# Three expert blocks, then three cosine blocks, with the operand differences made on GpSimd

## The chip, the cores and the metric

One core of a Trainium2 chip runs the whole program: windowed attention, a soft mixture of eight experts, and a feed-forward layer with a cosine gate. The metric is device time in microseconds (us). The engines are TensorE (PE in the rows; PEld is its weight load), VectorE (DVE), ScalarE (ACT), GpSimd (POOL) and SyncE (SP), which here issues the DMAs.

## The reference, cut to what matters

```python
# attention: B=4, H=8, S=576, D=64, causal window of 128, a slope per head
scores = np.where(mask, scale * q @ k.T + bias, -1e9)
x = softmax(scores) @ v            # reshaped to (2304, 512)
# experts: E=8, F=1024
P = np.exp(x @ w_gate - max)       # then 8 rounds: rows, columns normalised
for e in range(E):
    out += P[:, e:e+1] * (np.maximum(x @ w1[e], 0) @ w2[e])
# cosine layer: 512 -> 2048 -> 512; w_in and w_out come as float64
h = out @ w_in
return (h * np.cos(h)) @ w_out
```

## The kernel before

The 2304 tokens are three blocks (b = 0, 1, 2) of 768. A block goes through the experts in 32 units of 256 hidden columns ("moe"), and later through the cosine layer in 8 such units ("ffn"); a unit of a block is a step, and there are 120 steps. The texts call these expert blocks 0 to 2 and cosine blocks 0 to 2.

Every float32 operand is kept as a high part (a ScalarE copy rounded to the matmul's type) and a low part (what is left), and three products are summed. The front product of a unit (`g1`) is done in seven block products over halves of the operands, in the order B11, B21, T2, T1, T3, T4, B22 by the token operand that each reads (`ORDER`, `XI`). Each is six matmuls of 384 columns (`unit_mm`, L734). T1 = b12 - b11, T2 = b22 - T1, T3 = b22 - b12 and T4 = b21 - T2 are differences of quarters of the block; `combos` makes them (L264, VectorE) and splits all seven operands (L258 ScalarE, L259 VectorE) into the tiles `xt...`, of which there is one set. So the operands of the next block overwrite those of the running one, during its last step.

Within a unit the y bank accumulates four of the seven products, and is read out in between: ScalarE copies it into a snapshot (`keep`, L757) before the next product goes on accumulating; VectorE adds snapshots to the x and z banks (`add`, L760). An expert unit then applies relu and splits (L695 ScalarE, L696 VectorE); a cosine unit runs `cos_chain` over some two units' time (`tail`, one step at each `tick`), whose last operation is on GpSimd (L722). The output product (`g2`, L830 to L832) is six matmuls of 512 columns for each of six groups of 128 tokens; VectorE adds it into the block's sum (L811, L821).

The program is written out in order. The main loop goes over the steps; each step has seven positions j. At a position stand one front group, one `slot`, one output group of an earlier step with another `slot`, if one is due, and one piece of `combos` in the last step of a block. An expert step's output groups come at positions 1 to 6 of the next step; a cosine step's first comes at position 6 of the next, and its other five in the step after that. So the second unit of a cosine block holds one output group only, and the five are made up later.

Side work is fed in by slots, one piece of each list at a time: `pre` (the first block prepares the expert weights: `prep_s`, `prep_a`, `prep_b`, and stores them for the later blocks), `bg` (the normalisation of the gate; `x2_pieces`, the transposes that make a cosine block's operands from an expert block's sum; 32 times `convert_f64`, which turns a chunk of the float64 weights into float32 with seven VectorE operations, L218 to L238, and whose load buffer `u0` is single) and `bg2` (`prep_ffn`, the split of the cosine weights). Before a block's last step, `bg` and `bg2` are run to their end. In attention a list `conv` is stepped at every second group; the first block's `combos` is its last entry.

Buffers: `k0` to `k3` hold in turn a block's attention output, its expert sum, the cosine operands and the cosine sum.

## Time and profile before

| | us |
|---|---|
| median of 3 runs | 2176.64 |
| lowest and highest | 2174.65, 2178.61 |
| the profiled execution | 2179.0 |
| its span, first to last instruction | 2177.2 |

| engine | busy us | share of the span |
|---|---|---|
| TensorE | 2087.3 | 96% |
| VectorE | 1382.9 | 64% |
| ScalarE | 775.1 | 36% |
| GpSimd | 420.9 | 19% |

The share of an engine is an average over stages with different limits. The profile also gives the clock that TensorE was granted, as a share of its upper level: 1.00 is 2.4 GHz and 0.5 is 1.2 GHz; over the whole span it was 0.984. In the rows a line L734 is line 734 of the kernel above, "x6" counts instructions, and what stands in square brackets is the idle time of the engine just before the row, with who ended it.

### The profile page before, as it was taken

What the parts mean: (1) busy time and instruction counts of PE and PEld (TensorE: products, weight loads), DVE (VectorE), ACT (ScalarE), POOL (GpSimd) and SP (SyncE); (2) the same over time, 40 slices, a digit from 0 to 9 for tenths busy, and PEclk for the clock granted to TensorE, in tenths of its full rate; (3) what the DMA queues carried; (4) which work ended last, traced back from release to release, by engine and by line L of the source; (5) the groups of instructions that cost most, each with busy time, mean ns of one, the idle gap of its engine ahead of it and who ended that gap; (6) DMA issues with size and microseconds to landing.
All of it is one profiled execution on the core that took longest, in us unless ns stands there. A gap on an engine that the chain in (4) does not pass through costs nothing.

```text
span 2177.2 us, 28335 instructions
## 1 busy us (share of the span) xinstructions
PE 2087.3 (96%) x10623; PEld 1827.2 (84%) x10623; DVE 1382.9 (64%) x2497; ACT 775.1 (36%) x1544; POOL 420.9 (19%) x500
## 2 busy tenths in 40 slices
PE   8997999999999999999999499999999999899998
PEld 6665888988887888898988389888889898788897
DVE  5665866666787777777765357754545454656766
ACT  6774333333333222222223254312222222244443
POOL 4342233333332011122211212100000000022222
PEclk9998999999999999999999799999999999999999
DMA  5641567676776577878786535454444545444543
GB/s 142 156 115 66 196 247 260 240 267 240 272 271 254 200 270 289 307 280 312 290 296 232 200 153 202 169 192 177 173 199 168 205 164 209 159 169 185 189 163 117
DMA packets 162104, 456.94 MB, mean 210 GB/s; under 512 B 67504, under 2 KB 106416, under 8 KB 131248
## 3 DMA queue, kind: packets, MB, share of 16 engines
q1 hardware_dynamic: 161968, 455.15, 57.6%
q8 instruction: 83, 1.36, 0.3%
q14 instruction: 53, 0.43, 0.1%
HBM read 326.65 MB, written 128.45 MB: 209 GB/s over the span
## 4 chain that ended last, share of the span: by engine, by line
PE 79%; DVE 9%; ACT 4%; DMA 4%; POOL 3%; issue 1%; SPq 0%; POOLq 0%; ACTq 0%; DVEq 0%
PE y_moe L734 15%; PE g_moe L832 10%; PE g_moe L831 10%; PE g_moe L830 10%; PE z_moe L734 8%; PE y_ffn L734 4%; PE x_moe L734 3%; PE g_ffn L832 3%; PE g_ffn L831 3%; PE g_ffn L830 3%; PE s L427 3%; PE z_ffn L734 2%; PE x L519 2%; DMA wd<-wb 1%; ACT h_moe L695 1%
## 5 line engine op out<-in xcount | busy, mean ns | idle before, releaser
L821 DVE SCALAR_TENSOR_TENSOR acc_moe<-g_moe,prob,acc_moe 128x512 f32<-128x512 f32 x546 | 408.6, 748 | 278.4 <-PE g_moe L832 277.8
L832 PE MATMUL g_moe<-wb,h_moe 128*128 128x512 f32 x1152 | 459.7, 399 | 2.9 <-DVE h_moe L696 2.9
L830 PE MATMUL g_moe<-wb,h_moe 128*128 128x512 f32 x1152 | 451.5, 392 | 6.4 <-ACT h_moe L695 6.1
L831 PE MATMUL g_moe<-wb,h_moe 128*128 128x512 f32 x1152 | 456.4, 396 | 0.0
L757 ACT ACTIVATE s_moe<-y_moe 128x384 f32<-128x384 f32 x288 | 141.4, 491 | 687.7 <-PE y_moe L734 687.7
L734 PE MATMUL y_moe<-xtT_moe,wa 128*128 128x384 f32 x1728 | 352.7, 339 | 34.9 <-ACT s_moe L757 34.9
L734 PEld LDWEIGHTS y_moe<-xtT_moe,wa 128*128 128x128 f32 x1728 | 311.4, 190 | 62.5 <-ACT s_moe L757 38.2
L832 PEld LDWEIGHTS g_moe<-wb,h_moe 128*128 128x128 f32 x1152 | 216.8, 188 | 53.6 <-DVE h_moe L696 7.9
L722 POOL TENSOR_TENSOR h_ffn<-c_ffn,h_ffn 128x768 fp32r<-128x768 f32 x48 | 89.0, 1859 | 845.7 <-ACT h_ffn L720 813.0
L830 PEld LDWEIGHTS g_moe<-wb,h_moe 128*128 128x128 f32 x1152 | 217.6, 189 | 36.3 <-ACT h_moe L695 9.5
L695 ACT ACTIVATE h_moe<-c_moe 128x384 fp32r<-128x384 f32 x192 | 131.7, 686 | 310.3 <-DVE c_moe L760 309.4
L831 PEld LDWEIGHTS g_moe<-wb,h_moe 128*128 128x128 f32 x1152 | 216.9, 188 | 26.9
L696 DVE SCALAR_TENSOR_TENSOR h_moe<-c_moe,h_moe 128x384 fp32r<-128x384 f32 x192 | 146.8, 765 | 144.9 <-ACT h_moe L695 144.9
L120 POOL TENSOR_TENSOR s<-ra 128x256 f32<-128x256 f32 x80 | 60.5, 756 | 589.8 <-DVE wa L132 324.6
L760 DVE TENSOR_TENSOR c_moe<-z_moe,s_moe 128x384 f32<-128x384 f32 x192 | 106.9, 557 | 78.5 <-ACT s_moe L757 61.3
L734 PE MATMUL z_moe<-xtT_moe,wa 128*128 128x384 f32 x576 | 117.7, 339 | 0.0
L734 PE MATMUL y_moe<-xtB_moe,wa 128*128 128x384 f32 x576 | 116.7, 336 | 0.3
L734 PE MATMUL z_moe<-xtB_moe,wa 128*128 128x384 f32 x576 | 115.9, 336 | 0.0
L734 PE MATMUL x_moe<-xtB_moe,wa 128*128 128x384 f32 x576 | 115.8, 335 | 0.0
L830 PE MATMUL g_ffn<-wb,h_ffn 128*128 128x512 f32 x288 | 113.2, 393 | 2.3 <-DVE acc_ffn L811 2.3
L832 PE MATMUL g_ffn<-wb,h_ffn 128*128 128x512 f32 x288 | 114.5, 397 | 0.0
L811 DVE TENSOR_TENSOR acc_ffn<-g_ffn,acc_ffn 128x512 f32<-128x512 f32 x126 | 86.4, 688 | 44.2 <-PE g_ffn L832 43.4
(159 smaller groups left out, 3044.5 us busy)
## 6 DMA issues: line engine op xcount, KB each, us to landing
wa<-wd SPq DMA_DIRECT2D x88, 1792.0 KB, 8.7
wb<-wd SPq DMA_DIRECT2D x88, 1024.0 KB, 4.8
wd<-wa SPq DMA_DIRECT2D x32, 1792.0 KB, 6.8
wd<-wb SPq DMA_DIRECT2D x32, 1024.0 KB, 5.3
ra<-in_moe_w_dram SPq DMA_DIRECT2D x64, 256.0 KB, 7.4
rb<-in_moe_w_dram SPq DMA_DIRECT2D x64, 256.0 KB, 5.7
wd<-hla SPq DMA_DIRECT2D x48, 256.0 KB, 9.8
wd<-hlb SPq DMA_DIRECT2D x40, 256.0 KB, 8.4
```

What stands on the lines that cost most here:

```text
L427: nc.tensor.matmul(ps[:, x * 192 + c0:x * 192 + 192], qB[pi % 2][:, i, :], kT[pi][:, k0:k0 + w])
L695: nc.scalar.activation(out=h[:, 0, cols], in_=c, func=AF.Relu)
L696: nc.vector.scalar_tensor_tensor(out=h[:, 1, cols], in0=c, scalar=0.0, in1=h[:, 0, cols].bitcast(F32), op0=ALU.max, op1=ALU.subtract,)
L722: nc.gpsimd.tensor_tensor(out=h[:, 1], in0=c, in1=h[:, 0].bitcast(F32), op=ALU.subtract)
L734: nc.tensor.matmul(ps[:, :HB], wa[:, wl, WI[m], kc, :], x[:, xl, kc, :], start=start and kc == 0 and n_ == 0, stop=stop and kc == 1 and n_ ...
L757: nc.scalar.activation(out=snap[i], in_=y[:, :HB], func=AF.Copy)
L760: nc.vector.tensor_tensor(out=o, in0=ps[:, :HB], in1=snap[i], op=ALU.add)
L811: nc.vector.tensor_tensor(out=a, in0=ps, in1=a, op=ALU.add)
L821: nc.vector.scalar_tensor_tensor(out=a, in0=ps, scalar=pe, in1=a, op0=ALU.mult, op1=ALU.add)
L830: nc.tensor.matmul(ps, hf[f][:, 0, ts], wb[:, 0, f, :], start=f == 0, stop=False)
L831: nc.tensor.matmul(ps, hf[f][:, 0, ts], wb[:, 1, f, :], start=False, stop=False)
L832: nc.tensor.matmul(ps, hf[f][:, 1, ts], wb[:, 0, f, :], start=False, stop=f == 1)
```

## The change

The phases run in the order expert 0, 1, 2, cosine 0, 1, 2; before it was expert 0, 1, cosine 0, expert 2, cosine 1, 2. The buffers of sums and cosine operands follow. The differences move from VectorE to GpSimd, into a generator `stages` of their own: T1 and T2 are made four steps ahead of a block's end (a list `feed`), T3 and T4 together, right behind the split of T1, in place of T1 and T2. In attention, `stages` starts at group 46 and the splits at group 54, one piece at every group. The lists `bg` and `bg2` are not run to their end any more; only `feed` is. All 32 conversions are queued after the first step of expert block 1, where they follow each other without a break; before, one was queued at every step of that block, and six in the last twelve steps of block 0. The eight `prep_ffn` start every five steps, at steps 37 to 72.

```diff
+        def stages(b, src):
...
+            def stage(nm, i, x, y, over=None):
+                if over:
+                    t = st[over]
+                elif b in (("ffn", 1), ("ffn", 2)):
+                    t = rawp.tile([P, 4, P, 2], F32, tag=("ra", "rb")[i], name=f"st{nm}_{b[0]}{b[1]}")
+                    t = t.rearrange("p a f c -> p (a f c)")[:, :TB].rearrange("p (k f) -> p k f", k=2)
+                else:
+                    t = u_pool.tile([P, 2, HB], F32, tag=("u1", "u2")[i], name=f"st{nm}_{b[0]}{b[1]}")
+                nc.gpsimd.tensor_tensor(out=t, in0=x, in1=y, op=ALU.subtract)
+                st[nm] = t
+
+            stage("T1", 0, b12, b11)
+            yield
+            yield
+            stage("T2", 1, b22, st["T1"])
+            st["rest"] = lambda: (stage("T3", 0, b22, b12, "T1"), stage("T4", 1, b21, st["T2"], "T2"))
+            yield
+
+        def combos(b, src):
...
+            for nm in ("B11", "B21", "T2", "T1", "T3", "T4", "B22"):
...
                 nc.scalar.activation(out=t[:, 0], in_=s, func=AF.Copy)
                 nc.vector.tensor_tensor(out=t[:, 1], in0=s, in1=t[:, 0].bitcast(F32), op=ALU.subtract)
                 xt[b, nm] = t
-            def stage(i, x, y):
...
-                nc.vector.tensor_tensor(out=t, in0=x, in1=y, op=ALU.subtract)
...
+                if nm == "T1":
+                    st["rest"]()
+                yield
...
-            if n == 50:
-                conv.append(combos(("moe", 0), xr[0], u_pool, ("u0", "u1")))
+            if n == 46:
+                early.append(stages(("moe", 0), xr[0]))
+            if n == 54:
+                early.append(combos(("moe", 0), xr[0]))
+            if early and next(early[0], StopIteration) is StopIteration:
+                early.pop(0)
...
-        phases = [("moe", 0), ("moe", 1), ("ffn", 0), ("moe", 2), ("ffn", 1), ("ffn", 2)]
+        phases = [("moe", 0), ("moe", 1), ("moe", 2), ("ffn", 0), ("ffn", 1), ("ffn", 2)]
...
         def slot():
             step_all(pre)
+            step_all(feed)
             step_all(bg)
             step_all(bg2)
...
-            if nxt and nxt[0] == "ffn" and to_end == 3:
-                bg.append(x2_pieces(nxt[1]))
+            if nxt and to_end == 4:
+                if nxt[0] == "ffn":
+                    feed.append(x2_pieces(nxt[1]))
+                    feed.append(lazy(lambda nxt=nxt: stages(nxt, x2r[nxt[1]])))
+                else:
+                    feed.append(stages(nxt, xr[nxt[1]]))
             nx = None
             if last and nxt:
-                while bg or bg2:
-                    step_all(bg)
-                    step_all(bg2)
-                nx = combos(nxt, xr[nxt[1]] if nxt[0] == "moe" else x2r[nxt[1]], tp2, ("c1", "c2"))
+                while feed:
+                    step_all(feed)
+                nx = combos(nxt, xr[nxt[1]] if nxt[0] == "moe" else x2r[nxt[1]])
...
-            if kind == "moe" and (b == 1 or b == 0 and u >= 20 and u % 2) and chunk < 4 * NU2:
-                bg.append(convert_f64(chunk))
-                chunk += 1
-            if (kind, b) == ("moe", 1) and u >= 4 and (u % 4 == 0 or u == NU1 - 2):
-                bg2.append(prep_ffn(NU1 + (u - 4) // 4 + (u == NU1 - 2)))
+            if (kind, b) == ("moe", 1) and u == 0:
+                bg += [convert_f64(c) for c in range(4 * NU2)]
+            at = n - NU1
+            if 0 < at <= 5 * NU2 and at % 5 == 0:
+                bg2.append(prep_ffn(NU1 + at // 5 - 1))
```

The first place is ScalarE between the end of attention and the first unit of expert block 0. `lT` belongs to the gate, `xt...` are the split operands, `s1` is the unit's first snapshot. Before:

```order
L292 ACTIVATE lT4_2859<-gate4_2854 128x384
L292 ACTIVATE lT5_2866<-gate5_2861 128x384
L258 ACTIVATE xtB21_moe0_2878<-xr0_84 128x768
L258 ACTIVATE xtT2_moe0_2885<-st1_moe0_2883 128x768
L258 ACTIVATE xtT1_moe0_2888<-st0_moe0_2881 128x768
L258 ACTIVATE xtT3_moe0_2893<-st0_moe0_2891 128x768
L258 ACTIVATE xtT4_moe0_2898<-st0_moe0_2896 128x768
L258 ACTIVATE xtB22_moe0_2901<-xr0_84 128x768
L757 ACTIVATE s1_moe0_0_2952<-y_moe0_0_2941 128x384
```

And in the changed kernel:

```order
L299 ACTIVATE lT4_2883<-gate4_2878 128x384
L299 ACTIVATE lT5_2890<-gate5_2885 128x384
L773 ACTIVATE s1_moe0_0_2950<-y_moe0_0_2939 128x384
L773 ACTIVATE s2_moe0_0_2971<-y_moe0_0_2939 128x384
L325 ACTIVATE prob_80<-logits_81,nm_2975 128x144
```

The six splits that stood between the gate and the first snapshot are gone from there; they now stand among attention's groups.

The second place is VectorE in the last unit of expert block 2, before which the operands of a cosine block are made (before: cosine 1, now: cosine 0). `st` and `stT` are the differences, `c` the sums of snapshot and bank, `h` the relu's low half, `acc` the evacuated output. Before:

```order
L259 TENSOR_TENSOR xtB_ffn_16648<-x2r_16341,xtB_ffn_16648 128x768
L821 SCALAR_TENSOR_TENSOR acc_moe_13141<-g_moe_30_2_16657,prob,acc_moe_13141 128x512
L264 TENSOR_TENSOR st_ffn_16665<-x2r_16341 128x768
L264 TENSOR_TENSOR st_ffn_16667<-x2r_16341,st_ffn_16665 128x768
L259 TENSOR_TENSOR xtT_ffn_16669<-st_ffn_16667,xtT_ffn_16669 128x768
L760 TENSOR_TENSOR c_moe_31_16605<-z_moe_31_16603,s_moe_31_16680 128x384
L696 SCALAR_TENSOR_TENSOR h_moe_31_16679<-c_moe_31_16605,h_moe_31_16679 128x384
L821 SCALAR_TENSOR_TENSOR acc_moe_13141<-g_moe_30_3_16685,prob,acc_moe_13141 128x512
L259 TENSOR_TENSOR xtT_ffn_16693<-st_ffn_16665,xtT_ffn_16693 128x768
L696 SCALAR_TENSOR_TENSOR h_moe_31_16679<-y_moe_31_16601,h_moe_31_16679 128x384
L821 SCALAR_TENSOR_TENSOR acc_moe_13141<-g_moe_30_4_16704,prob,acc_moe_13141 128x512
L264 TENSOR_TENSOR st_ffn_16712<-x2r_16341 128x768
```

And in the changed kernel:

```order
L285 TENSOR_TENSOR xtB_ffn_15537<-x2r_15110,xtB_ffn_15537 128x768
L837 SCALAR_TENSOR_TENSOR acc_moe_11883<-g_moe_30_2_15546,prob,acc_moe_11883 128x512
L285 TENSOR_TENSOR xtT_ffn_15554<-stT_ffn_15244,xtT_ffn_15554 128x768
L776 TENSOR_TENSOR c_moe_31_15494<-z_moe_31_15492,s_moe_31_15565 128x384
L712 SCALAR_TENSOR_TENSOR h_moe_31_15564<-c_moe_31_15494,h_moe_31_15564 128x384
L837 SCALAR_TENSOR_TENSOR acc_moe_11883<-g_moe_30_3_15570,prob,acc_moe_11883 128x512
L285 TENSOR_TENSOR xtT_ffn_15578<-stT_ffn_15225,xtT_ffn_15578 128x768
L712 SCALAR_TENSOR_TENSOR h_moe_31_15564<-y_moe_31_15490,h_moe_31_15564 128x384
L837 SCALAR_TENSOR_TENSOR acc_moe_11883<-g_moe_30_4_15591,prob,acc_moe_11883 128x512
L285 TENSOR_TENSOR xtT_ffn_15599<-stT_ffn_15225,xtT_ffn_15599 128x768
L776 TENSOR_TENSOR c_moe_31_15493<-z_moe_31_15492,s_moe_31_15527 128x384
```

The three difference rows are off VectorE; the splits stand at the same places as before, between the same evacuations, and the split of T3 still stands ahead of the second add.

## Rows read from the trace of the kernel before

**Rows 1.** The page's first part: busy time, share of the span, instructions of TensorE.
```profile
PE 2087.3 (96%) x10623; PEld 1827.2 (84%) x10623; DVE 1382.9 (64%) x2497; ACT 775.1 (36%) x1544; POOL 420.9 (19%) x500
```

**Rows 2.** Who waited for whom, TensorE: total us, times, longest.
```profile
PE y_moe L734 <- ACT s_moe L757: 34.9, 7, 27.2
```

**Rows 3.** Stretches: length, each engine's busy us (instructions), clock, DMA share, GB/s.
```profile
1481.14:1840.86 359.72, 359.72 (x1796) 323.46 (x1795) 185.81 (x276) 76.81 (x139) 0.00 (x0) 1.00 0.47 185
182.50:205.06 22.56, 11.64 (x49) 10.46 (x49) 13.25 (x23) 6.78 (x11) 0.00 (x0) 0.70 0.07 24
553.63:667.86 114.23, 112.34 (x548) 98.00 (x546) 87.03 (x130) 41.20 (x71) 39.11 (x35) 1.00 0.74 266
683.50:726.04 42.54, 36.05 (x157) 30.27 (x156) 32.14 (x47) 13.22 (x21) 2.98 (x1) 0.92 0.54 198
1198.80:1278.60 79.80, 44.53 (x206) 38.55 (x204) 32.10 (x45) 26.11 (x47) 18.94 (x23) 0.81 0.51 183
1356.80:1395.97 39.17, 34.73 (x157) 30.44 (x156) 32.33 (x42) 18.35 (x27) 7.64 (x4) 0.91 0.41 150
1874.85:1926.21 51.36, 43.72 (x205) 37.83 (x204) 32.09 (x45) 18.38 (x29) 3.61 (x2) 0.93 0.44 172
2007.35:2045.74 38.39, 33.55 (x157) 29.46 (x156) 30.97 (x41) 18.77 (x27) 7.64 (x4) 0.96 0.41 153
```

**Rows 4.** Timeline, expert block 2 to cosine 1: start, length, engine, operation, idle before.
```profile
1885.04 0.96 DVE L264 TENSOR_TENSOR st_ffn<-x2r,st_ffn 128x768 f32<-128x768 f32 x1
...
1886.04 0.84 ACT L258 ACTIVATE xtT_ffn<-st_ffn 128x768 fp32r<-128x768 f32 x1 [5.18 <-DVE st_ffn L264]
...
1887.31 1.31 PE L734 MATMUL y_moe<-xtT_moe,wa 128*128 128x384 f32 x6 [1.52 <-ACT s_moe L757]
1887.78 0.55 DVE L760 TENSOR_TENSOR c_moe<-z_moe,s_moe 128x384 f32<-128x384 f32 x1
...
1890.07 0.95 DVE L259 TENSOR_TENSOR xtT_ffn<-st_ffn,xtT_ffn 128x768 fp32r<-128x768 f32 x1
...
1896.28 0.50 PE L830 MATMUL g_moe<-wb,h_moe 128*128 128x512 f32 x1 [1.74 <-ACT h_moe L695]
...
1900.78 0.69 PE L734 MATMUL y_ffn<-xtT_ffn,wa 128*128 128x384 f32 x1 [2.12 <-ACT s_ffn L757]
```

**Rows 5.** Timeline, last unit of cosine block 1: a VectorE product beside GpSimd.
```profile
2013.12 0.95 DVE L717 TENSOR_TENSOR c_ffn<-c_ffn,ta 128x768 f32<-128x768 f32 x1
...
2015.08 1.85 POOL L722 TENSOR_TENSOR h_ffn<-c_ffn,h_ffn 128x768 fp32r<-128x768 f32 x1 [10.11 <-ACT h_ffn L720]
2015.46 2.29 DVE L717 TENSOR_TENSOR c_ffn<-c_ffn,ta 128x768 f32<-128x768 f32 x1
```

**Rows 6.** Timeline, a float64 conversion's third-last operation, and the next load.
```profile
1000.20 0.69 DVE L234 SCALAR_TENSOR_TENSOR fb<-f,fb 128x512 f32<-128x512 uint32 x1
...
1000.92 0.88 SPq L203 DMA_DIRECT2D f<-in_moe_w_in_dram  x2
```

**Rows 7.** One line's instructions: issue to landing of L209's loads.
```profile
DMA to landing us min/median/max: 3.5/5.6/6.9
```

**Rows 8.** The same for L203's loads.
```profile
DMA to landing us min/median/max: 2.8/4.5/8.0
```

**Rows 9.** Timeline, attention: GpSimd and the matmul behind it.
```profile
88.30 2.36 POOL L145 TENSOR_TENSOR wb<-rb,wb 128x1024 fp32r<-128x1024 f32 x1
...
91.11 0.33 PE L482 MATMUL pt<-ident,pe 128*128 128x128 f32 x1 [0.54 <-POOL pe L469]
```

**Rows 10.** Timeline, front groups, relu's low half and its first reader.
```profile
977.16 1.21 PE L734 MATMUL y_moe<-xtB_moe,wa 128*128 128x384 f32 x6
...
977.44 0.96 DVE L696 SCALAR_TENSOR_TENSOR h_moe<-c_moe,h_moe 128x768 fp32r<-128x768 f32 x1 [0.91 <-ACT h_moe L695]
...
978.20 1.20 PE L734 MATMUL x_moe<-xtB_moe,wa 128*128 128x384 f32 x6
...
979.70 0.40 PE L832 MATMUL g_moe<-wb,h_moe 128*128 128x512 f32 x1
```

More of the change, by code (lines that the diff above doesn't have):

```diff
@@ L250, in tile_attention_moe_cos_ffn @@
         xt = {}
-        def combos(b, src, pool, tags):
+        stg = {}
+        def stages(b, src):
             b11, b12 = src[:, 0:2, :HB], src[:, 0:2, HB:]
             b21, b22 = src[:, 2:4, :HB], src[:, 2:4, HB:]
-            def split(nm, s):
+            st = {}
+            stg[b] = st
+            def stage(nm, i, x, y, over=None):
[15 more added lines that the diff above has]
+        def combos(b, src):
+            st = stg[b]
+            b11, b21, b22 = src[:, 0:2, :HB], src[:, 2:4, :HB], src[:, 2:4, HB:]
+            for nm in ("B11", "B21", "T2", "T1", "T3", "T4", "B22"):
+                s = {"B11": b11, "B21": b21, "B22": b22}.get(nm)
+                s = st[nm] if s is None else s
                 t = xtp.tile([P, 2, 2, HB], F32R, tag=f"xt{nm}", name=f"xt{nm}_{b[0]}{b[1]}")
@@ L260, in split @@
                 xt[b, nm] = t
-            def stage(i, x, y):
-                t = pool.tile([P, 2, HB], F32, tag=tags[i], name=f"st{i}_{b[0]}{b[1]}")
-                nc.vector.tensor_tensor(out=t, in0=x, in1=y, op=ALU.subtract)
-                return t
-            split("B11", b11)
-            yield
-            split("B21", b21)
-            yield
-            t1 = stage(0, b12, b11)
-            t2 = stage(1, b22, t1)
-            split("T2", t2)
-            yield
-            split("T1", t1)
-            yield
-            split("T3", stage(0, b22, b12))
-            yield
-            split("T4", stage(0, b21, t2))
-            yield
-            split("B22", b22)
-            yield
+                if nm == "T1":
+                    st["rest"]()
+                yield
         def gate_block(j, pool, sb):
@@ L592, in tile_attention_moe_cos_ffn @@
         conv = []
+        early = []
         NGR = len(groups)
@@ L642, in tile_attention_moe_cos_ffn @@
                 next_half += 1
-        for c in conv:
+        for c in conv + early:
             for _ in c:
@@ L662, in blk_tile @@
             return (blk2 if tag == "k3" else blk).tile(shape, F32, tag=tag, name=name)
-        phases = [("moe", 0), ("moe", 1), ("ffn", 0), ("moe", 2), ("ffn", 1), ("ffn", 2)]
-        acc_tag = {("moe", 0): "k3", ("moe", 1): "k0", ("ffn", 0): "k3", ("moe", 2): "k1",
-                   ("ffn", 1): "k0", ("ffn", 2): "k2"}
-        x2_tag = {0: "k1", 1: "k2", 2: "k3"}
+        phases = [("moe", 0), ("moe", 1), ("moe", 2), ("ffn", 0), ("ffn", 1), ("ffn", 2)]
+        acc_tag = {("moe", 0): "k3", ("moe", 1): "k0", ("moe", 2): "k1",
+                   ("ffn", 0): "k3", ("ffn", 1): "k0", ("ffn", 2): "k1"}
+        x2_tag = {0: "k2", 1: "k2", 2: "k2"}
         accs, x2r = {}, {}
-        bg, bg2, pre = [], [], []
+        bg, bg2, pre, feed = [], [], [], []
         def step_all(lst):
@@ L673, in step_all, with lazy @@
                 lst.pop(0)
+        def lazy(f):
+            yield from f()
         def slot():
             step_all(pre)
+            step_all(feed)
             step_all(bg)
@@ L866, in tile_attention_moe_cos_ffn @@
         bg.append(sinkhorn((p_m, "m"), skp))
-        chunk = 0
         load_f64(0)
```

## The prediction

> **What bounds the kernel now.** I read the page's first part, then who TensorE waits for, then a table of stretches cut at the starts of units, and then single boundaries on the timeline. TensorE is busy for 96% of the span [rows 1], so what can be won is the rest and whatever runs at the lower clock. A unit is 7 front groups and 6 output groups of six matmuls each. In the undisturbed part of the third expert block, 23 units take 359.72 us and TensorE is never idle [rows 3]: 15.64 us each. This is the floor, and nothing in the change touches it. The largest wait [rows 2] says what it waits for: 34.9 us on a snapshot that ScalarE copies out of the y bank, 27.2 of it at one place.
>
> The stretches [rows 3] price each place as its length less 15.64 per unit. Where a stretch holds the second unit of a cosine block, that unit has 1 output group and not 6; the five are done later, at 1.39 us each (15.64 less 7 front groups of 1.04 [rows 10], over 6), so 6.95 is added to the excess. Block 0 to 1: 42.54 - 31.28 = 11.3. Block 1 to cosine 0: 79.80 - 46.92 + 6.95 = 39.8. Cosine 0 to block 2: 39.17 - 31.28 = 7.9. Block 2 to cosine 1: 51.36 - 46.92 + 6.95 = 11.4. Cosine 1 to 2: 38.39 - 31.28 = 7.1. Together 77.5 us. Two more: the first unit takes 22.56 us, with TensorE busy for 11.64 at a mean clock of 0.70; and seven late units of expert block 0, where the float64 conversions start, take 114.23 - 109.48 = 4.8 too much.
>
> **The change, part by part.** All sums are against the profiled execution: span 2177.2, 2179.0 with what lies around it, which is 2.4 above the median of the runs, 2176.64.
>
> *Start of expert block 0.* Before, six of the seven operand splits and all four differences stand between attention's last ScalarE copy and the first snapshot; after, none does, as the first fence of the section on the change shows. The first unit then has 7 x 1.04 = 7.3 us of matmuls, the small ones of the normalisation, and one wait for a snapshot: I take 9.0, which needs the clock to stay at its upper level. Gain 13.6 (11 if the clock falls, 14.5 at best).
>
> The same work now runs inside attention: 7 copies of 0.84 on ScalarE, 7 differences of 0.95 on VectorE, and 4 GpSimd operations as long as the 1.85 us one of the same shape [rows 5]. Attention's normalisation is on GpSimd, and its matmuls wait for it: behind a 2.36 us GpSimd operation TensorE waited 0.54 us [rows 9]. T1 and T2 come alone, so 0.3 each. T3 and T4 come back to back, 3.7 us, of which 1.8 is hidden as there: 2. The splits I put at 0.2 each. Cost 4 (0 to 8).
>
> *Conversions out of expert block 0.* The 4.8 us go. Two GpSimd differences come into its 29th unit, behind the weight preparation: cost 1 (0 to 2).
>
> *Boundaries.* The flush is gone: the second preparation list starts at every fifth step, the last at step 72, and the cosine blocks begin at step 96, so nothing is left to flush. For the rest I replay block 2 to cosine 1 [rows 4]. Before, ScalarE stood 5.18 us at the T2 split, waiting for two VectorE differences; the snapshot behind it came late and TensorE idled 1.52. With T1 and T2 ready the two differences (0.95 each) and the copy of T2 (0.84) are no longer ahead of that snapshot, the add behind it (1887.78) comes 2.8 us earlier, and T1's split ends at 1891.02 - 2.8 = 1888.2. From there T3 is not faster: GpSimd takes 1.85, to 1890.2; ScalarE's copy 0.84, to 1891.1; but T4 holds GpSimd from 1890.2 to 1892.0. VectorE operations with both inputs in SBUF wait for a running GpSimd one: 0.95 us became 2.29 beside it [rows 5]. So T3's split runs 1892.0 to 1893.0, the add behind it to 1893.6, and ScalarE's relu to 1894.4. TensorE wants that at about 1892.9 (1896.28 less both gaps, and 0.1 for the ends that overlap): 1.5 idle, 0.5 more for the low half, and 0.5 for the next snapshot behind the splits of T4 and B22. That is 2.5 where there were 5.4.
>
> The Trainium skill, "SBUF — State Buffer", section "Who interferes with whom", states that a VectorE instruction with two SBUF inputs and a GpSimd instruction that reads SBUF exclude each other for the whole instruction. The trace agrees where it shows such a pair (0.95 against 2.29). Without this rule T3's split would start 0.9 earlier, and the five boundaries would cost 4.5 us less than I sum.
>
> The clock is the other part. Of the excess of 11.4 there, 51.36 - 43.72 = 7.6 is idle and the rest is the stretch at half clock (0.93 on average) [rows 3]. With gaps of 1.5 and 0.5 I expect half of that, 1.8. So 4.5 for block 0 to 1; 5 for block 1 to 2, where four GpSimd operations of a weight preparation stand ahead of T3; 6.5 for block 2 to cosine 0, which keeps the 2 us (7.6 - 5.4, rounded down) that a cosine block's thin second unit idles. Before, there were two such entries.
>
> Cosine to cosine, T2's split waits only for ScalarE's copy behind it, so the long snapshot wait nearly goes; VectorE's split still waits for the GpSimd half of the cosine, which holds the second half of the z bank for about 1 us. I take 2 each. Sum after: 20 (8 to 34). Gain 57.5.
>
> *Conversions in expert block 1.* 32 of them run end to end, one in 10 slots of the 13 in a unit, where there was one per unit. VectorE has room, but a conversion's first operation waits for its load, and the buffer is single. The load goes out when the third-last operation ends (1000.20 + 0.69, issued 1000.92) [rows 6]; the next first operation is due five slots on, 5 x 15.64 / 13 = 6.0 us from that operation's start, so 5.3 after the issue. Half of the chunks' loads land after 5.6 us in the middle and 6.9 at most, the others, in two pieces, after 4.5 and 8.0 [rows 7, 8]. VectorE will stand 0.3 us typically, 2.7 at worst, and behind it stand the evacuation and the adds. In the tightest place the low half is ready at 978.40 and wanted at 979.70: 1.3 us of slack [rows 10]. Most waits fit: cost 2 (0 to 6). The GpSimd differences in the middle of the cosine blocks delay VectorE once or twice: 1 (0 to 3). SyncE issues the same loads and stores as before, spread over expert blocks 1 and 2.
>
> **Sum.** -13.6 + 4 - 4.8 + 1 - 57.5 + 2 + 1 = -67.9; 2179.0 - 67.9 = 2111.1 profiled, 2.4 less as a median: **2109 us**. With all lower ends -88.8 (2088), with all upper ends -40.3 (2136).
>
> **Rivals.** *Clean boundaries* (20%): TensorE never waits for T3, the clock stays up, and attention hides the splits. Boundaries at 8 and attention at 2: 14 less, 2095. For it: both waits of ScalarE on T1 and T2 are gone, and only T3's chain is left. Against: the replay's 1.5 us behind T3.
>
> *Port-bound boundaries* (19%): every expert boundary keeps a clock drop and costs 8.5, a cosine one 5, so 37.5 with the thin unit instead of 20, and attention costs 8: 21.5 more, 2130. For it: T3 and T4 back to back block VectorE for 3.7 us where four differences took 3.8.
>
> *The work is not really ahead* (3%): prepared cosine weights are late and TensorE stops once for as long as the old flush, 27.2 us: 2136. Against: 20 units lie between.
>
> *Slower* (4%): VectorE waits for the float64 loads in expert block 1 at every conversion. Of each wait 1.3 us is slack; 31 waits eat the 68 us gained when each is 3.5 us, so from a landing of 8.8 us on. At 9.5 the wait is 4.2, and 31 x 2.9 = 90: 2109 - 2 + 90 = 2197. Against: 8.0 is the longest landing of all, with the 16 DMA engines three quarters busy late in block 0 (0.74, third of [rows 3]).
>
> **How the numbers follow.** 54% for the forecast, with its own range 2101 to 2120. The range for 8 in 10 takes in the clean case and most of the port-bound one: 2092 to 2130. Differences under 0.2% (4 us) cannot be told from none here. All cases but one end far below 2172, so faster 0.95, same 0.01, slower 0.04.
>
> **What would show it.** Right: no wait of TensorE above 5 us but the start; first unit near 9 us; no clock drop at the start of block 0; seven late units of block 0 at 15.64; at the expert boundaries no ScalarE wait on T2, and a TensorE gap of 1 to 2 us at the first output group behind the boundary, with VectorE's T3 split starting as GpSimd's T4 ends. Wrong: units of block 1 above 16 us with VectorE idle ahead of the conversion's first operation; attention longer by over 8 us; a boundary that idles as long as before.

## The result, and the profile after

The changed kernel takes 2155.15 us (median of 4 runs, 2153.53 to 2160.14) beside 2176.09 for the kernel before: a ratio of 0.9906, 95% interval 0.9887 to 0.9925. It is 21 us shorter (under 1%) where 68 were forecast, and lies outside the range of 2092 to 2130. The profiled execution has a span of 2154.0, so 23.2 of the span are gone and not 67.9.

The first part of the page after, for [rows 1]: TensorE is idle for less, 69 us in place of 90.

```profile
PE 2084.9 (97%) x10623; PEld 1816.9 (84%) x10623; DVE 1351.5 (63%) x2473; ACT 771.0 (36%) x1544; POOL 470.1 (22%) x524
```

Who TensorE waits for, for [rows 2] (total us, times, longest). The wait of 27.2 on the snapshot is gone. In its place stand many short waits, most of them for the relu and for the add that empties the z bank.

```profile
PE g_moe L846 <- ACT h_moe L711: 18.1, 14, 2.8
PE z_moe L750 <- DVE c_moe L776: 11.5, 10, 4.2
```

The stretches after, for [rows 3], in this order: the last seven units of expert block 0; its first unit; block 0 to 1; units 5 to 26 of block 1; block 1 to 2; block 2 to cosine 0; cosine 0 to 1; cosine 1 to 2. Columns as there: length, each engine's busy time, granted clock, DMA share, GB/s.

```profile
579.65:689.13 109.48, 109.48 (x547) 98.40 (x546) 71.33 (x106) 43.11 (x72) 39.61 (x35) 1.00 0.67 245
190.65:199.76 9.11, 8.53 (x50) 7.84 (x49) 4.12 (x13) 2.90 (x6) 0.00 (x0) 1.00 0.01 2
673.49:708.60 35.11, 33.38 (x157) 29.40 (x156) 24.00 (x32) 13.31 (x21) 6.07 (x3) 0.95 0.59 217
755.78:1143.19 387.41, 359.42 (x1717) 310.17 (x1716) 270.16 (x466) 83.93 (x177) 52.94 (x60) 0.99 0.72 263
1221.39:1257.82 36.43, 33.40 (x157) 29.40 (x156) 23.96 (x31) 13.34 (x25) 11.84 (x11) 0.95 0.57 217
1729.71:1774.79 45.08, 41.06 (x206) 36.34 (x205) 29.28 (x41) 19.59 (x30) 7.28 (x4) 1.00 0.50 197
1855.91:1891.09 35.18, 32.48 (x157) 27.84 (x156) 28.90 (x37) 18.78 (x27) 11.28 (x6) 1.00 0.48 174
1987.84:2023.01 35.17, 32.49 (x157) 27.83 (x156) 28.90 (x37) 18.77 (x27) 11.28 (x6) 1.00 0.47 173
```

Read as before, each length less 15.64 per unit. The seven late units have no excess, and nor have units 23 to 29, the stretch that [rows 3] has. The first unit takes 9.11. The boundaries cost 3.8, 5.2, 5.1 (45.08 - 46.92 + 6.95), 3.9 and 3.9, together 21.9. The fourth row is the surprise: 22 units take 387.41 where 22 x 15.64 = 344.08 would do, and TensorE is idle for 28.0 of it. Six units behind it, once the conversions are done, are at 15.64 again.

The sum over the places: attention 8.15 longer (it ends at 190.65 and not at 182.50), the first unit 13.45 shorter, the late units 4.8, the boundaries 55.6, block 1 42.7 longer (43.6 of excess, 0.9 before). That is -23.0, beside -23.2 measured.

VectorE's own waits from 690 to 1240 point to the cause. The first two are a conversion's first operation waiting for its float64 load, the third its fifth operation, which waits until the store before has left its buffer. Before, no conversion waited for either.

```profile
DVE fa L218 <- DMA f<-in_moe_w_in_dram: 31.8, 9, 6.7
DVE fa L218 <- DMA f<-in_moe_w_out_dram: 21.1, 7, 8.8
DVE fb L230 <- DMA w<-fb: 18.9, 6, 4.3
```

One such place on the timeline (start, length, engine, operation, idle before). SyncE issues 2.8 MB of weights (wb and wa), the raw weights of a cosine unit (ra and rb, four loads of 256 KB), and only then the float64 load. The load landed at 806.39, 11.8 us after its issue, and VectorE stood 8.79 us for it. The next add of the output and the one that empties the z bank stood behind.

```profile
791.03 0.32 SPq L109 DMA_DIRECT2D wb<-wd  x1
791.40 0.43 SPq L109 DMA_DIRECT2D wa<-wd  x1
791.88 1.22 SPq L88 DMA_DIRECT2D ra<-w  x2
793.15 0.96 SPq L88 DMA_DIRECT2D rb<-w  x2
794.55 0.33 SPq L209 DMA_DIRECT2D f<-in_moe_w_out_dram  x1
...
806.49 0.43 DVE L218 TENSOR_SCALAR fa<-f 128x512 int32<-128x512 int32 x1 [8.79 <-DMA f<-in_moe_w_out_dram]
```

Two more places that the prediction spoke of. At block 0 to 1, ScalarE no longer waits for T2, and T3's chain is what ends last: GpSimd makes T3 and T4 one after the other, VectorE's split of T3 takes 1.71 beside T4, and the gap at the first output group is 1.46.

```profile
686.97 1.85 POOL L267 TENSOR_TENSOR stT_moe<-xr 128x768 f32<-128x768 f32 x1 [8.25 <-DVE xtT_moe L285]
688.78 1.86 POOL L267 TENSOR_TENSOR stT_moe<-xr,stT_moe 128x768 f32<-128x768 f32 x1
689.74 1.71 DVE L285 TENSOR_TENSOR xtT_moe<-stT_moe,xtT_moe 128x768 fp32r<-128x768 f32 x1 [1.72 <-ACT xtT_moe L284]
...
692.85 0.50 PE L846 MATMUL g_moe<-wb,h_moe 128*128 128x512 f32 x1 [1.46 <-ACT h_moe L711]
```

In attention the same two operations stand ahead of the softmax's normalisation (L476), and TensorE waits 4.21 for it. The granted clock fell to its lower level during that wait (0.51 on average from 138 to 145).

```profile
134.02 1.80 POOL L267 TENSOR_TENSOR stT_moe<-xr 128x768 f32<-128x768 f32 x1 [1.81 <-DVE ars L470]
135.78 1.80 POOL L267 TENSOR_TENSOR stT_moe<-xr,stT_moe 128x768 f32<-128x768 f32 x1
...
137.57 1.64 POOL L476 TENSOR_SCALAR pe<-pe,arr 128x192 f32<-128x192 f32 x1
...
139.26 0.48 PE L489 MATMUL pt<-ident,pe 128*128 128x128 f32 x1 [4.21 <-POOL pe L476]
```

### The profile page after: what moved, and what is told of

Same layout as the page of the kernel before. It is cut to its first block, busy times and chain, and to the rows that moved or that the text cites. A ratio compares the mean times of both kernels' runs of the same rounds, so it can differ in the third digit from the quotient of the medians.

```text
span 2154.0 us, 28332 instructions
## 1 busy us (share of the span) xinstructions
PE 2084.9 (97%) x10623; PEld 1816.9 (84%) x10623; DVE 1351.5 (63%) x2473; ACT 771.0 (36%) x1544; POOL 470.1 (22%) x524
## 5 line engine op out<-in xcount | busy, mean ns | idle before, releaser
L120 POOL TENSOR_TENSOR s<-ra 128x256 f32<-128x256 f32 x80 | 59.5, 743 | 717.0 <-DMA ra<-w 401.8
L750 PEld LDWEIGHTS z_moe<-xtB_moe,wa 128*128 128x128 f32 x576 | 103.5, 191 | 23.9 <-DVE c_moe L776 16.5
L846 PE MATMUL g_ffn<-wb,h_ffn 128*128 128x512 f32 x288 | 113.0, 392 | 2.3 <-DVE acc_ffn L827 2.3
```

The lines of the kernel that those rows point to most:

```text
L120: nc.gpsimd.tensor_tensor(out=s4[:, o], in0=x, in1=y, op=op)
L750: nc.tensor.matmul(ps[:, :HB], wa[:, wl, WI[m], kc, :], x[:, xl, kc, :], start=start and kc == 0 and n_ == 0, stop=stop and kc == 1 and n_ ...
L846: nc.tensor.matmul(ps, hf[f][:, 0, ts], wb[:, 0, f, :], start=f == 0, stop=False)
```

## The experiments

### What makes expert block 1 longer

**One conversion per unit.** Theory A: the loads come too late for end-to-end conversions. B: the new order of the phases. C: the density of VectorE's work. In the new order a conversion's two work tiles become the staging tiles of expert block 2 from unit 29 on, so 27 conversions fit in block 1 and five follow in block 2.

```diff
-            if (kind, b) == ("moe", 1) and u == 0:
-                bg += [convert_f64(c) for c in range(4 * NU2)]
+            if kind == "moe" and (b == 1 and u < 27 or b == 2 and 1 <= u < 6):
+                bg.append(convert_f64(u if b == 1 else 26 + u))
```

> The changed kernel with the conversions one per unit again (27 in the units 1 to 27 of expert block 1, the last 5 in units 2 to 6 of expert block 2); everything else as changed. In the changed kernel block 1 took 547.9 us, 43.6 of it above 15.64 per unit in its units 3 to 25, and VectorE stood 53 us at the first operation of conversions, waiting for float64 loads, and 19 us at the fifth, waiting for the store before. Theory A (end-to-end conversions come back to the single float64 buffer before the load has landed, and VectorE stands there with adds and evacuations queued behind it): with 13 slots per conversion VectorE gets there 9.5 us after the load's issue, loads land after 3.5 to 8.4, so no wait is left; block 1 takes 505 (boundary 3.8 and at most 1), total 2113 (2108 to 2118). Rival B (phase order: block 1 loses its time to weight preparation or loads that now stand in it, not to conversions): block 1 stays above 535, total 2145 to 2155. Rival C (density of VectorE work itself) also gives 2113 here; the other runs tell it from A.

2114.48 (2112.2 to 2116.73), ratio 0.9713 (0.9692 to 0.9734). Block 1 takes 502.7. Its 22 units at the place of the row above, one row of the same view:

```profile
755.74:1099.82 344.08, 344.08 (x1718) 309.27 (x1717) 251.98 (x419) 87.09 (x176) 48.51 (x60) 1.00 0.77 281
```

Not one idle moment in 344.08 us, with DMA engines that are busier than in the changed kernel (0.77, 0.72). B falls. A and C both forecast this; the next runs tell them apart.

**The end-to-end conversions alone, in the kernel before.**

```diff
-            if kind == "moe" and (b == 1 or b == 0 and u >= 20 and u % 2) and chunk < 4 * NU2:
-                bg.append(convert_f64(chunk))
-                chunk += 1
+            if (kind, b) == ("moe", 1) and u == 0:
+                bg += [convert_f64(c) for c in range(4 * NU2)]
```

> The kernel before with one part of the change alone: all 32 float64 conversions end to end from the first unit of expert block 1, none in block 0; phase order, flush and operand differences as before. Theory A and rival C: the late units of block 0 lose their 4.8 us of excess, block 1 grows by about 40 us in its first 25 units, VectorE waits for float64 loads by about 50 us in total: 2212 (2200 to 2222). Rival B (the loss needs the new phase order): block 1 stays as before, 2170 to 2175.

2209.63 (one run), slower than before by 34, as A and C have it. VectorE's waits appear with it, in a kernel where all else is as before:

```profile
DVE fa L218 <- DMA f<-in_moe_w_in_dram: 25.7, 7, 5.9
DVE fa L218 <- DMA f<-in_moe_w_out_dram: 19.8, 9, 5.0
DVE fb L230 <- DMA w<-fb: 18.1, 6, 5.5
```

**No float64 loads but the first.** The other 31 loads are left out, and all conversions work on the first chunk.

```diff
+            if c:
+                f64_t[c] = f64_t[c - 1]
+                return
             raw = u_pool.tile([P, 512, 2], I32, tag="u0", name=f"f64_{c}")
 ...
-            raw = f64_t.pop(c)
+            raw = f64_t[c]
```

> The changed kernel with only the first float64 chunk loaded: the other 31 loads are left out, and every conversion works on the first chunk's data (so the weights of the cosine blocks are not the reference's). All operations on VectorE and all stores stay, end to end in 10 slots. Theory A: no wait at the first operation, at most a few for the stores; units of block 1 at 15.64 to 16, its excess falls from 43.6 to 5 (0 to 10), total 2116 (2110 to 2121). Rival C (density itself, VectorE busy for 75 per cent of block 1): excess stays above 30, total 2141 to 2153.

2121.45 (one run). TensorE is idle for 4.0 us from 709 to 1127, and block 1 takes 512.2, 9.4 more than with one conversion per unit. So of the 43 us the density costs at most 9, and in those there is still the wait for the store:

```profile
709.00:1127.00 418.00, 414.02 (x2049) 367.79 (x2048) 318.85 (x540) 100.14 (x203) 57.76 (x66) 1.00 0.66 243
```

```profile
DVE fb L233 <- DMA w<-fb: 13.0, 6, 3.8
```

C falls as the main cause. VectorE is busy for 318.85 of 418 us there, and that alone does not stop TensorE. In units 1 to 30 of block 1 the excess is 7.9 us beside 13.0 of waits for the store; in the changed kernel it is 43.6 beside 71.8 of waits (31.8 + 21.1 + 18.9). Both are about 0.6 us of time for each us that VectorE waited, so hardly anything is left for density to explain.

**Eleven slots in place of ten.**

```diff
             load_f64(c + 1)
             yield
             yield
+            yield
```

> The changed kernel with one empty slot more per conversion between the load's issue and the next conversion's first operation: 11 slots in place of 10, still end to end. Theory A: VectorE comes to the first operation about 1.2 us later after the load's issue (median 4.6 to about 5.8; loads land after 3.5 to 11.8, median 5.4), and has 1.2 us more per conversion to recover; the waits fall to less than half of 72 us, and the excess of block 1 from 43.6 to 15 (8 to 25): total 2126 (2118 to 2138). Rival C (density of VectorE work): the work per unit falls by one eleventh, excess 39, total 2150 (2145 to 2155).

2146.65 (2145.13 to 2148.37), where A had 2126 (up to 2138) and C 2150 (2145 to 2155): the time is in C's range and misses A's. The waits fell from 71.8 to 48.3 us, not to less than half:

```profile
DVE fb L230 <- DMA w<-fb: 18.3, 6, 7.0
DVE fa L218 <- DMA f<-in_moe_w_out_dram: 16.7, 6, 6.7
DVE fa L218 <- DMA f<-in_moe_w_in_dram: 13.3, 5, 4.6
```

The run without the loads leaves C no such cost, so A lacked something: why some loads land so late. I set each load's landing beside the time since the last 1.8 MB weight load was issued. In the changed kernel 16 loads went out less than 6.5 us behind one, and landed after 7.2 us on average and 11.8 at most; 30 went out later and landed after 4.3 on average. With one conversion per unit all 46 went out 7.4 to 8.0 behind one. The weight load itself took 8.7 to 12.1 us to land there. Conversions of 10 or 11 slots drift against units of 13, and meet the weight load again and again, at places where more of it is still to come.

**The loads on another queue.** Is it SyncE's queue, where the load stands behind the weights, or the DMA engines that both share?

```diff
-                    nc.sync.dma_start(
+                    nc.gpsimd.dma_start(
 ...
-                nc.sync.dma_start(out=raw.rearrange("p n t -> p (n t)"), in_=w_out[r0:r0 + P, :])
+                nc.gpsimd.dma_start(out=raw.rearrange("p n t -> p (n t)"), in_=w_out[r0:r0 + P, :])
```

> The changed kernel (conversions end to end, 10 slots) with one thing moved: the float64 loads are issued from GpSimd's queue in place of SyncE's. Theory A2, formed on the runs so far: end-to-end conversions drift against the units, and a load that SyncE issues less than 6.5 us after a unit's 1.8 MB weight load lands behind that, after 7.2 us on average and up to 11.8, where one issued later lands after 4.3 (16 and 30 loads of the changed kernel); at one per unit every load went out 7.4 to 8.0 us after the weight load. On a queue of its own it need not stand behind: landing at most 7, VectorE's waits for loads fall from 53 to 20 or less, total 2127 (2115 to 2140). Rival F (not the queue but the 16 DMA engines, busy with the weights, make the load late): landings and waits as in the changed kernel, total 2148 to 2160.

2170.57 (one run), worse than the changed kernel and above both forecasts. The loads that start less than 6.5 us behind a weight load (23 now) land after 7.7 on average and 11.4 at most, from a queue of their own; the others after 4.9. That is 2.9 later for the near ones, as on SyncE's queue. VectorE waits longer:

```profile
DVE fa L218 <- DMA f<-in_moe_w_in_dram: 56.1, 12, 7.7
...
DVE fa L218 <- DMA f<-in_moe_w_out_dram: 30.6, 10, 6.4
```

VectorE waits for no store in this run: 86.7 us of waits, all for loads, go with an excess of 59.1 in units 1 to 30. So late loads alone are enough. The queue falls as the main cause. What is left is the time of the start. The Trainium skill, "DMA: Bandwidth & Descriptors", section "Issuing engines are not separate DMA queues", says that transfers run on the same 16 engines and interleave, whichever engine starts them; this run agrees (7.2 and 7.7).

**The same rate at another phase.** One conversion per unit, each begun 9 slots later in its unit.

```diff
             if (kind, b) == ("moe", 1) and u == 0:
-                bg += [convert_f64(c) for c in range(4 * NU2)]
+                bg.append(pause(9))
+            if kind == "moe" and (b == 1 and u < 26 or b == 2 and 1 <= u < 7):
+                bg.append(convert_f64(u if b == 1 else 25 + u))
```

(pause yields 9 times; each conversion has three empty slots at its end, so that it fills a unit.)

> The kernel with one conversion per unit (2114.5), with every conversion begun 9 slots later in its unit, at the same rate (13 slots each). There the float64 loads went out 7.4 to 8.0 us behind a weight load's issue and landed after 4.9 on average, 7.9 at most. Theory F2 (formed on the queue's run: a float64 load that starts while a 1.8 MB weight load is under way shares the 16 DMA engines with it and lands late, from whatever queue): now most go out 2 to 6 us behind it, and land after 6.5 to 7.5 on average, 10 to 12 at most; VectorE gets there after 9.5, so waits of VectorE stay under 10 us in total and the time under 2120. Rival C2 (loads are late because VectorE's work is dense, not for where they start): landings as in the one-per-unit kernel, 4.5 to 5.5 on average.

2114.76 (one run). Of 46 loads 37 now go out 4.8 to 5.8 us behind the weight load. These land after 6.9 on average, the other nine after 5.0, all together after 6.5; with the first phase it was 4.9. Issue to landing of L203's and L209's loads in this kernel (the longest with the first phase were 7.5 and 7.9):

```profile
DMA to landing us min/median/max: 3.3/5.9/10.1
DMA to landing us min/median/max: 5.3/6.2/10.1
```

VectorE gets there 8.7 us after the issue in the middle, so it waits 3.4 us in all and the time stays. C2 falls: phase makes the landing late, and the short way from load to use makes that cost.

The weight load is not the whole of it. Where the four raw loads of a cosine unit stand between it and the float64 load, that one lands later still: after 8.9 on average here (8 of the 37 loads; 6.4 for the other 29), and after 10.1 in the changed kernel (3 of 16; 6.5 for the other 13). On GpSimd's queue they made no difference (7.7 for the 3 loads behind them, 7.7 for the other 20), so for this part the common queue may count. No run moved the raw loads alone.

### What the boundaries and attention wait for

All six start from the kernel with one conversion per unit (2114.48; profiled span 2110.6, attention until 190.5, boundaries 22.0).

**T4 one step later.**

```diff
-                if nm == "T1":
-                    st["rest"]()
+                if nm in ("T1", "T3"):
+                    st[nm + "rest"]()
```

(T1rest makes T3, T3rest makes T4.)

> The kernel with one conversion per unit (2114.5), with T4's difference issued one step later than T3's, so that in attention the normalisation of another group stands between the two on GpSimd. Theory D (attention loses its time because two differences back to back, 3.6 us, hold GpSimd while TensorE waits for the normalisation behind them, and the clock falls): the 4.2 us wait of TensorE there becomes 2.4 or less, no fall of the clock, attention 4.5 shorter (2 to 6). At the block boundaries GpSimd has nothing between the two, so T4 still follows T3 at once and VectorE's split of T3 still takes 1.7: boundaries unchanged. Total 2110 (2108 to 2113). Rival G (the two also come apart at the boundaries, since the later place in the program holds T4 back): the split takes 0.95, five boundaries give 1.5 each as well, 2103.

2112.25 (2111.81 to 2112.62). Attention ends at 190.3: D falls in this form. TensorE's first wait became shorter (1.23), but at the next group it waited 2.84 for a softmax operation that stood behind VectorE's split of T3, which took 2.48 beside T4. At the boundaries T4 still follows T3 at once and the split takes 1.70, as expected: GpSimd has nothing else there, and a later place in the program holds nothing back.

**T3 and T4 on VectorE.**

```diff
-                nc.gpsimd.tensor_tensor(out=t, in0=x, in1=y, op=ALU.subtract)
+                (nc.vector if over else nc.gpsimd).tensor_tensor(out=t, in0=x, in1=y, op=ALU.subtract)
 ...
+                if nm == "T4":
+                    st["T4go"]()
 ...
                 if nm == "T1":
-                    st["rest"]()
+                    st["T1go"]()
```

(T1go makes T3, T4go makes T4.)

> The kernel with one conversion per unit (2114.5), with T3 and T4 made by VectorE (T3 right behind T1's split, T4 at its own split), T1 and T2 ahead on GpSimd as changed. Theory P (at a boundary the end is set by T3: GpSimd's 1.85, ScalarE's copy, then a VectorE split that stands while GpSimd makes T4): T3 takes 0.95, its split 0.95 in place of 1.7, so it ends 1.6 earlier (3.5 at block 1 to 2, where four weight preparations stand ahead on GpSimd); TensorE's gap of 1.5 to 3.3 at the first output group goes or stays under 0.5, each expert boundary costs 0.5 to 2 and each cosine one 2 to 3, together 12 in place of 22; attention is 6.5 shorter, with no GpSimd operation of 1.8 behind which the normalisation stands. Total 2098 (2093 to 2104). Rival V (VectorE is short at the boundary: the differences that it makes push the relu's low half and the adds back by as much): boundaries 20 to 24, total 2106 to 2110.

2118.38 (2118.01 to 2122.6): slower, where 2098 was expected, and above V's 2106 to 2110 too. Block 1 to 2 shows why:

```profile
1200.65 0.50 PE L849 MATMUL g_moe<-wb,h_moe 128*128 128x512 f32 x1 [1.10 <-ACT h_moe L714]
...
1203.15 0.84 ACT L287 ACTIVATE xtT_moe<-stT_moe 128x768 fp32r<-128x768 f32 x1 [2.55 <-DVE stT_moe L267]
...
1205.16 1.33 PE L753 MATMUL y_moe<-xtT_moe,wa 128*128 128x384 f32 x3 [2.31 <-ACT s_moe L776]
```

The wait behind T3 fell from 3.3 to 1.1, but ScalarE now stood 2.55 for T4, and the snapshot behind it came late: 2.31. A wait was exchanged for another. Attention ended at 194.8, with 3 us of it lost before the first edited operation, part of that at another fall of the clock (0.79 from 110 to 115, where the kernel that it starts from has 1.00); those 3 us are not the edit's.

**T3 on VectorE, T4 on GpSimd already behind T2's split.**

```diff
-                nc.gpsimd.tensor_tensor(out=t, in0=x, in1=y, op=ALU.subtract)
+                (nc.vector if nm == "T3" else nc.gpsimd).tensor_tensor(out=t, in0=x, in1=y, op=ALU.subtract)
 ...
-                if nm == "T1":
-                    st["rest"]()
+                if nm in ("T1", "T2"):
+                    st[nm + "go"]()
```

(T1go makes T3, T2go makes T4.)

> The kernel with one conversion per unit (2114.5), with T3 made by VectorE right behind T1's split, and T4 by GpSimd already behind T2's split (issued ahead of T1's step). With both on VectorE the first wait behind a boundary was gone (1.45 to 0, 3.32 to 1.10), but T4 stood 2.5 us ahead of ScalarE's copy and the next snapshot came 2.3 late. Theory P2: with T4 ready early neither wait is left; the boundaries cost 14 in place of 22 and the total is 2106 (2102 to 2110). Rival V2 (T4 on GpSimd now holds VectorE's split of T1, as it held T3's before): the wait only moves, boundaries 20 to 22, 2111 to 2115.

2108.27 (2107.72 to 2110.16), ratio 0.9695 (0.9673 to 0.9718): the fastest kernel here, 47 us under the changed one. The boundaries cost 1.3, 4.9, 4.1, 3.5 and 4.5, together 18.3, where 14 was expected. At block 0 to 1 the gap is down from 1.45 to 0.52. At block 1 to 2 two weight preparations (L120) stand ahead of T4, so that T4 starts just ahead of VectorE's split of T1, which takes 2.65 in place of 0.95 and ends 0.83 behind T4. V2 holds there. Attention ends at 188.4, 2.1 earlier, and the first unit takes 10.7, 1.6 more.

```profile
1187.50 1.85 POOL L267 TENSOR_TENSOR stT_moe<-xr,stT_moe 128x768 f32<-128x768 f32 x1
1187.53 2.65 DVE L286 TENSOR_TENSOR xtT_moe<-stT_moe,xtT_moe 128x768 fp32r<-128x768 f32 x1
...
1195.09 0.50 PE L847 MATMUL g_moe<-wb,h_moe 128*128 128x512 f32 x1 [2.60 <-ACT h_moe L712]
```

**One step in every second group of attention**, and this together with the last:

```diff
-            if early and next(early[0], StopIteration) is StopIteration:
+            if early and n % 2 == 0 and next(early[0], StopIteration) is StopIteration:
```

> The kernel with one conversion per unit (2114.5), with one step of the differences and splits of expert block 0 in every second group of attention in place of every group. Attention ends at 190.5 there and at 182.5 before. Theory S (seven splits and four differences in neighbouring groups take VectorE, ScalarE and GpSimd more than the slack of the softmax chain, TensorE idles and the clock falls behind it): spread over twice the groups most of it fits, attention ends at 185 (183 to 187), total 2109 (2106 to 2112). Rival H (each step costs what it costs, wherever it stands, since the chain has no slack): attention 189 to 192, total 2112 to 2116.

> Both edits: T3 on VectorE with T4 early on GpSimd, and the spread in attention. They act in different places, so by P2 and S the gains add: 2101 (2097 to 2106). By V2 and H none is left: 2112 to 2116.

2112.93 (2111.71 to 2115.98) and 2110.04 (2108.22 to 2110.88): attention ends at 192.0 and 190.5. H holds, spreading gains nothing, and both edits together miss the 2101 that P2 and S had. TensorE's waits in the first of the two stand at the splits, for a softmax operation of VectorE (L446) that stands behind one, and once, in the last row, behind T3 and T4 on GpSimd:

```profile
127.80 0.92 PE L434 MATMUL s<-kT,qB 128*128 128x192 f32 x4 [1.29 <-DVE anb L446]
133.10 0.92 PE L434 MATMUL s<-kT,qB 128*128 128x192 f32 x4 [0.93 <-DVE anb L446]
137.92 0.44 PE L398 MATMUL T<-ident,qr 128*128 128x128 f32 x2 [0.96 <-DVE anb L446]
142.72 0.92 PE L434 MATMUL s<-kT,qB 128*128 128x192 f32 x4 [0.62 <-DVE anb L446]
145.55 0.33 PE L489 MATMUL pt<-ident,pe 128*128 128x128 f32 x1 [1.70 <-POOL pe L476]
```

**The splits behind attention again**, with T1 and T2 alone inside it.

```diff
-            if n == 54:
-                early.append(combos(("moe", 0), xr[0]))
 ...
-        for c in conv + early:
+        for c in conv + early + [combos(("moe", 0), xr[0])]:
```

> The kernel with one conversion per unit (2114.5), with the seven splits of expert block 0 and its T3 and T4 put back behind attention; only T1 and T2 stay ahead, inside it. Spread or not, on GpSimd or VectorE, attention has ended at 188 to 192 with all of them inside it, and TensorE waits 0.6 to 1.3 us at several of the splits for a softmax operation that stands behind one on VectorE. Theory S2 (each split costs attention about 0.9, T3 with T4 the rest): attention ends at 184 (183 to 185.5), 6 earlier; the first unit, with T1 and T2 ready, takes 18 (16 to 21) in place of 9.1; total 2117 (2114 to 2121). Rival H2 (it is T1 and T2, or weight preparation met at another time, that make attention longer): attention still ends at 188 or later, total 2120 to 2126.

2115.37 (2111.58 to 2116.91). Attention, and then the first unit, in the view of stretches:

```profile
0.00:182.98 182.98, 171.44 (x1172) 119.02 (x1172) 109.12 (x555) 128.81 (x430) 82.65 (x188) 0.99 0.53 136
182.98:202.79 19.81, 12.26 (x49) 10.74 (x50) 11.00 (x20) 7.36 (x12) 3.57 (x2) 0.66 0.00 1
```

S2 holds: T1 and T2 cost attention 0.5, the splits with T3 and T4 the other 7.5. Moving them ahead saves 10.7 in the first unit and costs 7.5 in attention, 3 net in these profiles; the medians of the two kernels (2115.37 and 2114.48) do not tell them apart.

## Why the prediction was wrong

- **First unit**: 9.0 forecast, 9.11 measured, with no fall of the clock. Right, and so were the **conversions out of block 0**: the seven late units are at 15.64. The two terms of 1 us for GpSimd differences inside blocks measured nothing.
- **Boundaries**: 20 forecast, 21.9 measured; one by one 4.5, 5, 6.5, 2, 2 against 3.8, 5.2, 5.1, 3.9, 3.9. At the expert boundaries the mechanism was the one replayed: T3's split beside T4 (1.71), a gap of 1.5 and another of 0.3. The rule of the Trainium skill that was weighed there ("SBUF — State Buffer", section "Who interferes with whom") agrees with this split, 1.71 where 0.95 is its own time. The cosine ones were put too low: their last units still have 1.5 of excess and the first ones 2.4. That the sum comes so close is in part luck: the entry into the cosine blocks was put 1.4 too high, and the two cosine boundaries 1.9 too low each.
- **Attention**: 4 forecast, 8.15 measured, just past the upper end. The term that was mis-sized is "the splits I put at 0.2 each": TensorE's waits at them are 0.6 to 1.3 (the rows above), and T3 with T4 cost 4.2 in one wait, not 2. The stretch of attention, before and after, shows that all of it is idle time of TensorE: 10.5 us became 19.2, and its busy time did not grow. The rows at hand showed one GpSimd operation, and none showed a VectorE operation of 0.95 in the middle of the softmax chain.

```profile
0.00:182.50 182.50, 172.02 (x1172) 119.86 (x1173) 108.86 (x556) 129.40 (x430) 78.78 (x186) 0.99 0.53 134
0.00:190.65 190.65, 171.48 (x1172) 118.95 (x1173) 115.66 (x562) 133.16 (x435) 86.97 (x190) 0.98 0.51 131
```

- **Conversions in expert block 1**: 2 (0 to 6) forecast, 42.7 measured. This step failed, and it carries 40.7 of the 44.9 us between the forecast sum and the measured one: with one conversion per unit the same kernel takes 2114.5, beside 2109 forecast. Three things were wrong in it. First, "half of the chunks' loads land after 5.6 us in the middle and 6.9 at most" was read from a kernel in which every load that follows a 1.8 MB weight load goes out at least 7.4 us behind it. End to end they drift over it, to 3.0 us behind it, and landings reach 11.8. Second, "5.3 after the issue" is counted from five slots of mean length, and the places in a unit are not alike. (The operation that frees the buffer is the sixth of seven, not the third-last; the count of slots is right.) VectorE reached the first operation from 2.4 to 6.4 us after the issue, 4.6 in the middle, and soonest where the load was latest: after 3.3 on average at the ten conversions whose load went out less than 6.5 us behind a weight load, after 5.2 at the others. In nine of the ten it had worked from the issue on with at most 0.9 us of idle time. These ten make 45.0 of the 52.9 us of waits for loads. A wait does not bring on the next: after a conversion with more than 1 us of waits VectorE arrived after 4.7 on average, after the others after 4.5. Third, the work tile's store (18.9 us of waits) was not in the sum at all. A store lands after up to 11.4 us, and VectorE was back at its tile after 6.4 at the earliest; in the kernel before it was back after 12.4 at the earliest, and stores landed after 7.8 at most.
- The rival *slower* had this mechanism, with its point of decision at landings of 8.8 us at every conversion. It takes less: waits at 16 of the 31 conversions and six waits for the store cost 43 us. Its ground against, "8.0 is the longest landing of all", was a fact about the old schedule. Its price, each wait less 1.3 us of slack, comes near: 71.8 us in 22 waits give 43.2 here, where 43.6 were measured (58.1 and 59.1 with the loads on GpSimd's queue; with eleven slots 26.2, where 32.2 were measured). What makes up the cost is another thing: in the 22 units of the fourth row TensorE was idle for 28.0 us of the 43.3, and the other 15.3 are the edges of 39 gaps (about 10 us, last section) and the lower clock (about 4).
- Two of the prediction's own signs of being wrong came: units of block 1 above 16 us with VectorE idle ahead of a conversion's first operation, and attention longer by over 8 us (8.15).

What stays open: the waits for loads and for stores were not priced apart by a run of their own. By the 0.6 us for each us of wait that the run without loads and the changed kernel share, the stores' 18.9 us would be about 11 of the 43.6, an estimate. A second buffer for the loads was not tried. Nor is it shown why VectorE works without a break where the unit changes, which makes the way from load to use short there.

## What to carry to other kernels

A landing time is a property of the moment at which a transfer starts, not of the transfer: when a change moves a load, price it by what else is under way at its new places, with the longest landing behind large loads as the upper bound. When side work is packed end to end through one buffer, look at the shortest way from load to use over all the places that the drift will reach (2.4 us here), and not at the mean one (5.3). And work moved ahead into another stage is paid there by the chain that has no slack: most of what the first unit gained went back in attention (8.15 of 13.45 in all; 7.5 of 10.7 for the splits, T3 and T4).

## What the runs showed of the hardware

- A float64 load of 512 KB or two of 256 KB that starts less than 6.5 us behind a 1.8 MB load landed after 7.2 us on average (4.3 otherwise); from another queue it was 7.7 (4.9 otherwise). With four raw loads of 256 KB in between on the same queue (three of the 16) it was 10.1.
- A gap on TensorE costs about 0.26 us beyond its idle time, at the full granted clock. In an unbroken row, matmuls of 512 columns start 0.23 us apart and are listed as 0.39 to 0.40 long (their ends are modelled), so they overlap. Ahead of a gap the last one runs out with no other beside it; behind it the first is 0.50 long and the next starts 0.34 later, and the ones after that are 0.23 apart again. The 39 gaps in units 5 to 26 of block 1 in the changed kernel cost about 10 us so, by the starts of their matmuls. One of them:

```profile
831.87 0.50 PE L846 MATMUL g_moe<-wb,h_moe 128*128 128x512 f32 x1 [0.50 <-ACT h_moe L711]
832.21 0.39 PE L847 MATMUL g_moe<-wb,h_moe 128*128 128x512 f32 x1
```

- A VectorE split of 0.95 took 1.71 beside a GpSimd difference of 1.86, and 2.65 beside one of 1.85 that had started just before it. It ended 0.81 and 0.83 us behind the GpSimd operation, wherever it had started; so did the product of [rows 5] (2.29, 0.82 behind).
